# Chunk 0's reciprocal taken from VectorE in two halves, PSUM cleared by ScalarE, and a new order of all tasks, in a gated linear-attention and squared-ReLU kernel

## The chip, the cores and the metric

One core of a Trainium2 chip runs the whole program. The metric is the time of one execution in device microseconds; 338.8 us is the median of three runs before the change (338.04 to 339.99).

The engines are named as the profile names them: PE is TensorE (matmuls; PEld its weight loads), DVE VectorE, ACT ScalarE, POOL GpSimd, and SP the engine whose queue issues nearly all loads and stores.

## The reference

Two stages, for 4 batches of 768 tokens. First a gated linear attention with 8 heads of 48: a state per head decays by f and takes up k times v. Then a token mix, a squared-ReLU pair of products (384 to 1024 to 384), and a sigmoid gate.

```python
f = 1.0 / (1.0 + np.exp(-f_logit))
for t in range(S):
    state = f[:, :, t, :, None] * state + np.einsum('bhd,bhe->bhde', k[:, :, t], v[:, :, t])
    y[:, :, t] = np.einsum('bhd,bhde->bhe', q[:, :, t], state)
# x is y, heads side by side; x_prev is x one token earlier
xk = mu_k * x + (1.0 - mu_k) * x_prev
xr = mu_r * x + (1.0 - mu_r) * x_prev
k = np.maximum(xk @ w_k, 0.0)
out = 1.0 / (1.0 + np.exp(-(xr @ w_r))) * (k * k @ w_v)
```

## The kernel before

The attention is done in 24 chunks of 128 tokens (6 per batch). The rest is done in 8 units of 3 chunks (384 tokens).

For chunk i the tasks are, by the names that the order uses: `qk` and `v` load q, k and v; `b` is a scan over the tokens that gives the running product of the gates, in PSUM (tag pm), and `bl` keeps its last column. `ln` and `rb` (ScalarE, Ln and then Exp of its negative) give 1/b roughly, `n` and `iv` (VectorE) improve it by one Newton step, which leaves it with a negative sign. `q` multiplies q by b (VectorE), `k` multiplies k by minus 1/b in two operations of 256 columns (GpSimd or VectorE). `S` is the scores k times q (16 small matmuls into pss), `m` and `mg` copy and mask them, `TR` and `kt` transpose k and copy it to SBUF, `P` is k times v. `g`, `za`, `zb` and `T` carry the state from chunk to chunk: `g` is the gate of the whole last chunk, `za` the decayed state, `zb` and `T` add the two parts of P. `YA`, `YB` are the output's matmuls (into py) and `y` copies them, times -1, to x and stage; `w` is a small copy between YA and YB.

The work of unit u: `sp` spreads rows of two heads by DMA, `d`, `xm`, `xh`, `xl` mix the token with the one before and split it in two float32r parts; for unit 0, chunks 0 to 2, the mix is done on TensorE instead (`XM`, with the diagonal matrices dg and eg, which come from mu). `F` is a block of the first product (9 matmuls), `r`, `h`, `kk`, `l` square and split it, `R` and `lg` the gate's product, `sg` its sigmoid, `W` a block of the second product (12 matmuls, four blocks of the hidden width each), `o` the gated output, `out` its store. The weights come as 64-bit words and are made into float32r pairs on the chip, each piece in steps S, T, X, H, L (as `wkS0`), from the loads `wk0` to `wk7`, `wr0` to `wr3`, `wv0` to `wv5`.

At the end the kernel checks that nothing it has simplified matters: `c0` to `c14` load the weights' words again through two buffers, `cm` gathers them, `lo` reduces on VectorE, `lot` turns the result on TensorE (two transposes), `lom` makes a flag of it in four small VectorE operations, and `strong` reads the flag on every engine for a branch to a general version, not taken here.

What sets the order: a long string, ORDER, names all tasks in one sequence, with the engine after a slash where there is a choice. Each engine does its own tasks in this sequence. Buffers are given out in this sequence as well. `constants` and the clears ahead of it come first.

Of the kernel before, what the change touches and what calls it, by code (L numbers as in the profile page):

```python
# [51 lines left out]
f0.0 f0.1 sf0.0 b0 mu wv3 f0.2 sf0.1 sf0.2 f1 b1 sf1 ex wvS3/V wvT3 onemu wvX3 b2 bl0/V qk0 v0 qk1 bl2/A q0 bl1/V g2  # L52
dg/G b3 q1 ln0 rb0 ln1 bl3/V rb1 n0 iv0 wv2 qk2 n1 q2 iv1 k0/G k1/G wvS2/A qk3 q3 wvT2 wk0 ed2 v2 v1 wk4 S0 ln2 rb2
m0/A n2 wvX2 iv2 TR0 kt0/A wkS0/A S1 P0 zb0/A ln3 m1/A TR1 YA0 w0/A wkT0 wkX0 kt1/A rb3 T0 mg0/G g1 YB0 k2/G za1/G b4
n3 y0/A P1 S2 TR2 zb1 YA1 wk5 wk2 wk1 qk4 v3 ed0 ed1 wk6 wk3 iv3 T1 ln4 wkS5/A bl4/A m2/V wvH3/G mg1/G za2/G wkS2/A
kt2/A wkH0/A P2 rb4 w1/A wkS1/A wkT2 mg2/V wkT5 wkX2 q4 zb2 YB1 n4 T2 wkX5 wkT1 k3/G wkL0/G x00 wvH2/G g3 wkH5/G g4
# [119 lines left out]
class Rwkv:  # L176
# [10 lines left out]
    def b(self, *key):  # L187
        return self.tiles[key[0]][self.slot[key]]
# [12 lines left out]
    def add_attention(self, pl, i):  # L201
# [35 lines left out]
        def halves(t):  # L237
            return t[:, 1::2].rearrange("p a (h c) -> p a h c", h=2)
# [784 lines left out]
```

## Time and profile before

| | us |
|---|---|
| median of 3 runs | 338.8 |
| lowest, highest | 338.04, 339.99 |
| the profiled execution: own time | 339.45 |
| the profiled execution: span | 337.7 |
| TensorE busy | 309.6 (92%) |
| VectorE busy | 271.9 (81%) |
| ScalarE busy | 200.1 (59%) |
| GpSimd busy | 141.3 (42%) |

The profiled execution is one execution of the program. Its span is what the rows below show; 1.75 us of its own time lie around the span. The clock granted to TensorE was 0.998 of full speed over the span. An idle engine costs something only where another one, or the end, waits for it.

### The profile page before, as it was taken

The numbers are of one execution on the slowest core, as the hardware profiler recorded it, in microseconds if no ns is written. First come the engines' busy times: TensorE is split into PE (matmuls) and PEld (weight loads), VectorE is DVE, ScalarE is ACT, GpSimd is POOL, SyncE is SP. The second block draws the span as 40 slices with busy tenths as digits, with TensorE's granted clock in tenths as the row PEclk, the third lists the DMA queues.
The fourth block names the chain that finished last, engine by engine and source line by source line (L and its number), as shares of the span: only waits on it lengthen the run. The fifth ranks groups of instructions, "written<-read, shape, count | busy, mean of one in ns | idle before, by whom it ended". The sixth has DMA issues, their size and how long they took to land.

```text
span 337.7 us, 10736 instructions
## 1 busy us (share of the span) xinstructions
PE 309.6 (92%) x4458; PEld 296.5 (88%) x4458; DVE 271.9 (81%) x519; ACT 200.1 (59%) x427; POOL 141.3 (42%) x184
## 2 busy tenths in 40 slices
PE   0097989999999999999999999999999999999993
PEld 0076779999999998999999999999999999999893
DVE  8988889998799967599988958888889997663751
ACT  3786779776788246675975425656782532914150
POOL 2488878934426704231374424051434331113340
PEclk9999999999999999999999999999999999999999
DMA  7997949620025229300060607620065021326423
GB/s 246 384 264 237 318 127 411 214 107 2 1 90 170 92 53 365 120 1 2 14 203 22 209 2 215 199 82 0 2 211 156 4 64 48 112 68 213 136 99 105
DMA packets 20634, 45.32 MB, mean 134 GB/s; under 512 B 2848, under 2 KB 13024, under 8 KB 20576
## 3 DMA queue, kind: packets, MB, share of 16 engines
q1 hardware_dynamic: 20144, 43.96, 39.6%
q8 instruction: 37, 0.61, 0.8%
q10 hardware_dynamic: 432, 0.59, 0.5%
q14 instruction: 21, 0.17, 0.2%
HBM read 38.54 MB, written 4.72 MB: 128 GB/s over the span
## 4 chain that ended last, share of the span: by engine, by line
PE 82%; DMA 8%; DVE 3%; issue 3%; SPq 1%; POOL 1%; ACT 0%; DVEq 0%; POOLq 0%
PE pm L453 63%; PE py L334 8%; DMA qk<-in_qkt 4%; PE pss L302 4%; PE pm L287 3%; DMA words<-in_wk 3%; PE pm L583 2%; PE pss L321 2%; DMA out<-t 1%; DVE pm L525 1%; DVE t L545 1%; SPq L381 0%; POOL dg L761 0%; DVE dg L748 0%; DVE t L507 0%
## 5 line engine op out<-in xcount | busy, mean ns | idle before, releaser
L453 PE MATMUL pm<-xh,wk 128*128 128x384 f32 x384 | 104.8, 339 | 0.5 <-DVE t L629 0.5
L453 PE MATMUL pm<-wv,k2h 128*128 128x384 f32 x384 | 97.0, 333 | 0.4 <-DVE t L545 0.3
L453 PEld LDWEIGHTS pm<-xh,wk 128*128 128x128 f32 x384 | 69.3, 188 | 2.4 <-DVE t L629 0.8
L453 PEld LDWEIGHTS pm<-wv,k2h 128*128 128x128 f32 x384 | 68.3, 188 | 1.2 <-DVE t L545 0.6
L453 PE MATMUL pm<-wv,k2l 128*128 128x384 f32 x192 | 63.6, 331 | 0.0
L453 PE MATMUL pm<-xl,wk 128*128 128x384 f32 x192 | 63.6, 331 | 0.0
L635 POOL TENSOR_TENSOR k2l<-t,k2h 128x384 fp32r<-128x384 f32 x36 | 39.1, 1097 | 57.3 <-ACT k2h L627 44.7
L560 POOL TENSOR_TENSOR xl<-t,xh 128x384 fp32r<-128x384 f32 x25 | 26.4, 1064 | 59.8 <-ACT xh L553 42.6
L453 PE MATMUL pm<-wr,xh 128*128 128x384 f32 x144 | 36.5, 334 | 0.0
L453 PEld LDWEIGHTS pm<-xl,wk 128*128 128x128 f32 x192 | 36.1, 188 | 0.0
L453 PEld LDWEIGHTS pm<-wv,k2l 128*128 128x128 f32 x192 | 36.0, 188 | 0.0
L627 ACT ACTIVATE k2h<-t 128x384 fp32r<-128x384 f32 x64 | 32.5, 521 | 5.8 <-DVE t L623 5.6
L622 ACT ACTIVATE t<-pm 128x384 f32<-128x384 f32 x37 | 17.7, 489 | 30.6 <-PE pm L453 28.4
L302 PE MATMUL pss<-qk 64*64 64x64 f32 x768 | 17.2, 228 | 17.4 <-POOL qk L241 16.2
L302 PEld LDWEIGHTS pss<-qk 64*64 64x64 f32 x768 | 14.5, 141 | 18.4 <-POOL qk L241 16.2
L223 DVE TENSOR_TENSOR_SCAN pm<-f,low 128x512 f32<-128x512 f32 x24 | 30.2, 1262 | 0.2
L453 PEld LDWEIGHTS pm<-wr,xh 128*128 128x128 f32 x144 | 25.5, 188 | 0.2
L241 POOL TENSOR_TENSOR qk<-qk,rb 128x256 f32<-128x256 f32 x17 | 13.7, 806 | 27.2 <-DVE rb L246 27.1
L366 ACT ACTIVATE x<-py 64x128 f32<-64x128 f32 (+1 forms) x63 | 19.5, 309 | 9.1 <-PE py L334 8.1
L553 ACT CAST xh<-t 128x384 fp32r<-128x384 f32 x32 | 15.9, 511 | 14.9 <-DVE t L545 14.8
L545 DVE SCALAR_TENSOR_TENSOR t<-pm,mu_sb,x 128x384 f32<-128x384 f32 x42 | 24.2, 609 | 0.4
L453 PE MATMUL pm<-wr,xl 128*128 128x384 f32 x72 | 23.9, 332 | 0.0
(127 smaller groups left out, 597.9 us busy)
## 6 DMA issues: line engine op xcount, KB each, us to landing
qk<-in_qkt SPq DMA_DIRECT2D x24, 512.0 KB, 5.2
words<-in_wv SPq DMA_DIRECT2D x12, 512.0 KB, 5.0
f<-in_zt SPq DMA_DIRECT2D x7, 768.0 KB, 6.7
v<-in_vt SPq DMA_DIRECT2D x24, 192.0 KB, 3.8
out<-t SPq DMA_DIRECT2D x21, 192.0 KB, 4.1
words<-in_wk SPq DMA_DIRECT2D x6, 512.0 KB, 3.9
words_k2h<-in_wk SPq DMA_DIRECT2D x4, 384.0 KB, 6.4
words_k2l<-in_wk SPq DMA_DIRECT2D x4, 384.0 KB, 5.9
```

The lines of the kernel that those rows point to most:

```text
L223: pl.add(f"b{i}", ("V", lambda: nc.vector.tensor_tensor_scan(b().rearrange(FL), f().rearrange(FL), self.low.rearrange(FL), 1.0, op0=ALU.mu ...
L241: e.tensor_tensor(k()[:, ::2], k()[:, ::2], rb()[:, ::2], op=ALU.mult)
L302: nc.tensor.matmul(self.pss[HALF[h], r, 64 * j : 64 * j + 64], k()[HALF[r], j, HALF[h]], q()[HALF[r], j, HALF[h ^ j % 2]], start=True, sto ...
L334: first[c, h] = nc.tensor.matmul(to, lhs, rhs, start=(c, h) not in first, stop=stop, skip_group_check=True)
L366: e.activation(o, i_, AF.Copy, scale=-1.0)
L453: nc.tensor.matmul(lines(ps), lhs(a, j), lines(rhs(bb, j)), start=ends[0] and i == 0, stop=ends[1] and i == len(pr) - 1)
L545: pl.add(f"xm{u}.{p}{w}{j}", ("V", lambda xm=xm, w=w, j=j: nc.vector.scalar_tensor_tensor(xm(), pm("d", u, p, j), self.mu_sb[:, w, j : j + ...
L553: pl.add(f"xh{u}.{p}{w}{j}", ("A", lambda xm=xm, hi=hi: nc.scalar.copy(hi(), xm())), ("V", lambda xm=xm, hi=hi: nc.vector.tensor_copy(hi() ...
L560: e.tensor_tensor(lo(), xm(), hi().bitcast(F32), op=ALU.subtract)
L622: pl.add(f"r{name}", ("A", lambda: nc.scalar.activation(r(), ps(), AF.Relu)), ("V", lambda: nc.vector.tensor_scalar(r(), ps(), 0.0, None, ...
L627: pl.add(f"h{name}", ("A", lambda: nc.scalar.activation(hi(), r(), AF.Square)), after=[f"r{name}"], **(kw | {"uses": kw["uses"] + [("t", " ...
L635: e.tensor_tensor(lo(), kk(), hi().bitcast(F32), op=ALU.subtract)
```

## The change

For chunk 0 the running product b goes to SBUF (the tile lg, which is free at the start) instead of PSUM. Its reciprocal is taken by VectorE's own reciprocal, in two halves of two head pairs (`ra0`, `rb0`); `ln0`, the Exp, `n0` and `iv0` are gone. k's product follows in two halves on GpSimd (`ka0`, `k0`), of two operations with 128 columns each. Since this reciprocal has a positive sign, q of chunk 0 is negated first (`nq0`, ScalarE), and the gate of chunk 1 is negated (`g1`, now on VectorE). The scores of chunk 0 are two tasks (`Sa0`, `S0`) with two head pairs each. Two clears of PSUM that were memsets on VectorE are copies of zeros on ScalarE. ORDER is another string: 1407 words for 1406.

```diff
-        b = lambda: self.b("pm", ("b", i)).rearrange("p (a c) -> p a c", a=NP)
+        home = ("lg", "b0") if i == 0 else ("pm", ("b", i))
...
+            def turned(e):
+                e.scalar_tensor_tensor(g(), self.bl[:, 0], -1.0, f()[:, :, 0], op0=ALU.mult, op1=ALU.mult)
...
-        pl.add(f"S{i}", ("P", scores), after=I("q") + I("k") + I("m", i - 1))
+        if i == 0:
+            pl.add("Sa0", ("P", lambda: scores((0, 1))), after=["q0", "ka0"])
+            pl.add("S0", ("P", lambda: scores((2, 3))), after=["Sa0", "k0"])
+        else:
+            pl.add(f"S{i}", ("P", scores), after=I("q") + I("k") + I("m", i - 1))
...
+    def add_first(self, pl, q, k, b, rb, home):
+
+        nc = self.nc
+        pl.add("nq0", ("A", lambda: nc.scalar.activation(q(), q(), AF.Copy, scale=-1.0)), after=["qk0"])
+        pl.add("q0", ("G", lambda: nc.gpsimd.tensor_tensor(q(), q(), b(), op=ALU.mult)),
+               ("V", lambda: nc.vector.tensor_tensor(q(), q(), b(), op=ALU.mult)), after=["nq0"], uses=[home])
+        for n, js in (("ra0", slice(0, 2)), ("rb0", slice(2, 4))):
+            pl.add(n, ("V", lambda js=js: nc.vector.reciprocal(rb()[:, js].rearrange(FL), b()[:, js].rearrange(FL))),
+                   uses=[home] + ([("rb", 0)] if js.start else []), takes=[] if js.start else [("rb", 0)])
+
+        def k_rb(e, j):
+            e.tensor_tensor(k()[:, j], k()[:, j], rb()[:, j], op=ALU.mult)
+            t, r = (a[:, j + 1].rearrange("p (h c) -> p h c", h=2) for a in (k(), rb()))
+            e.tensor_tensor(t, t, r[:, ::-1], op=ALU.mult)
+
+        for n, j, ra in (("ka0", 0, "ra0"), ("k0", 2, "rb0")):
+            pl.add(n, ("G", lambda j=j: k_rb(nc.gpsimd, j)), ("V", lambda j=j: k_rb(nc.vector, j)),
+                   after=["qk0", ra] + (["ka0"] if j else []), uses=[("rb", 0)])
...
-    nc.vector.memset(k.py[:, :, :320], 0.0)
-    nc.vector.memset(k.pss[:, :, 256 : 256 + NP * D], 0.0)
+    zeros = k.eg.rearrange("p m j c -> p (m j c)")
+    for t, n in ((k.py[:, :, :320], 320), (k.pss[:, :, 256 : 256 + NP * D], NP * D)):
+        nc.scalar.copy(t, zeros[:, : 2 * n].rearrange("p (h c) -> p h c", h=2))
...
-f0.0 f0.1 sf0.0 b0 mu wv3 f0.2 sf0.1 sf0.2 f1 b1 sf1 ex wvS3/V wvT3 onemu wvX3 b2 bl0/V qk0 v0 qk1 bl2/A q0 bl1/V g2
+f0.0 sf0.0 f0.1 f0.2 sf0.1 f1 b0 qk0 b1 bl0/A sf0.2 sf1 nq0 ex ra0 b2 ka0/G rb0 k0/G TR0 bl1/A kt0/A ln1 rb1 q0/V v0 wv3 mu onemu qk1 b3 q1 n1 v1 qk2
```

Three places in the new order matter for what follows. In the rows below the first word is the line in each kernel, numbers behind names are buffers, and f, qk, words and pm stand for gates, q and k, weight words and PSUM.

VectorE near the start, before: from the scan of chunk 2 (L223) over q0 and q1 (L233) to the Newton steps n and iv of chunks 0 and 1 (L244, L246).

```order
L223 SCALAR_TENSOR_TENSOR pm_96<-f_61,low 128x512
L227 COPY bl<-pm_93 128x4
L233 TENSOR_TENSOR qk_64<-qk_64,pm_93 128x512
L227 COPY bl<-pm_94 128x4
L223 SCALAR_TENSOR_TENSOR pm_95<-f_62,low 128x512
L233 TENSOR_TENSOR qk_65<-qk_65,pm_94 128x512
L227 COPY bl<-pm_95 128x4
L244 TENSOR_TENSOR pm_93<-rb_97,pm_93 128x512
L246 SCALAR_TENSOR_TENSOR rb_97<-pm_93,rb_97 128x512
L244 TENSOR_TENSOR pm_94<-rb_98,pm_94 128x512
L233 TENSOR_TENSOR qk_66<-qk_66,pm_96 128x512
L246 SCALAR_TENSOR_TENSOR rb_98<-pm_94,rb_98 128x512
```

The same engine from its first scan in the changed kernel: scans (L228), the two reciprocals, q0 (L397), one minus mu (L794), q1, n1, T0 (L270) and iv1.

```order
L228 SCALAR_TENSOR_TENSOR lg_121<-f_61,low 128x512
L228 SCALAR_TENSOR_TENSOR pm_93<-f_61,low 128x512
L399 RECIPROCAL rb_97<-lg_121 128x256
L228 SCALAR_TENSOR_TENSOR pm_94<-f_61,low 128x512
L399 RECIPROCAL rb_97<-lg_121 128x256
L397 TENSOR_TENSOR qk_64<-qk_64,lg_121 128x512
L794 TENSOR_SCALAR one_mu<-mu_sb 128x6
L228 SCALAR_TENSOR_TENSOR pm_96<-f_62,low 128x512
L374 TENSOR_TENSOR qk_65<-qk_65,pm_93 128x512
L385 TENSOR_TENSOR pm_93<-rb_98,pm_93 128x512
L270 TENSOR_TENSOR sm<-pss,z_73 128x192
L387 SCALAR_TENSOR_TENSOR rb_98<-pm_93,rb_98 128x512
```

The Newton step of chunk 0 and three small copies have left this stretch; the reciprocals stand around the scan of chunk 2, one_mu stands between q0 and the scan of chunk 3, and T0 has come up ahead of iv1.

SP's queue of loads at the start, before:

```order
L381 DMA f_61<-in_zt 128x512 x2
L755 DMA mu_sb<-in_mu 128x6
L666 DMA words_122<-in_wv 128x1024
L381 DMA f_61<-in_zt 128x512
L381 DMA f_62<-in_zt 128x1536
L211 DMA qk_64<-in_qkt 128x1024
L213 DMA v_103<-in_vt 128x384
L211 DMA qk_65<-in_qkt 128x1024
```

And in the changed kernel:

```order
L419 DMA f_61<-in_zt 128x512 x3
L419 DMA f_62<-in_zt 128x1536
L211 DMA qk_64<-in_qkt 128x1024
L213 DMA v_103<-in_vt 128x384
L704 DMA words_122<-in_wv 128x1024
L793 DMA mu_sb<-in_mu 128x6
L211 DMA qk_65<-in_qkt 128x1024
L213 DMA v_104<-in_vt 128x384
```

The load of mu and the first piece of w_v have moved behind q, k and v of chunk 0.

TensorE near the program's end, before: the two transposes of the check (L789) and the read of the flag (L800), with the first and last rows of the one block of 12 matmuls between them, and the first of the block behind.

```order
L789 MATMUL pm_94<-ident,t_114 1x128 x2
L453 MATMUL pm_93<-wv_86,k2h_891 128x3x32x4
...
L453 MATMUL pm_93<-wv_86,k2l_978 128x3x32x4
L800 TENSOR_LOAD flag
L453 MATMUL pm_95<-wv_86,k2h_891 128x3x32x4
```

The same place in the changed kernel, with the last two matmuls of block W7.00 ahead:

```order
L491 MATMUL pm_96<-wv_87,k2h_846 128x3x32x4
L491 MATMUL pm_96<-wv_86,k2l_857 128x3x32x4
L827 MATMUL pm_95<-ident,t_114 1x128 x2
L838 TENSOR_LOAD flag
L491 MATMUL pm_94<-wv_86,k2h_846 128x3x32x4
L491 MATMUL pm_94<-wv_87,k2h_846 128x3x32x4
```

The read of the flag now follows the transposes directly, and four blocks (48 matmuls) stand behind it, where one stood before.

## Rows read from the trace of the kernel before

**Rows 1.** The page, part 1: busy us (share of span) x instructions.
```profile
PE 309.6 (92%) x4458; PEld 296.5 (88%) x4458; DVE 271.9 (81%) x519; ACT 200.1 (59%) x427; POOL 141.3 (42%) x184
```

**Rows 2.** Busy us by stretch: stretch, length, PE, PEld, DVE, ACT, POOL, clock, DMA, GB/s.
```profile
10.00:20.00 10.00, 3.58 (x84) 2.95 (x88) 9.21 (x17) 8.20 (x13) 6.66 (x9) 1.00 0.92 334
20.00:30.00 10.00, 7.16 (x251) 5.79 (x243) 8.43 (x18) 8.22 (x25) 8.37 (x13) 1.00 0.84 255
...
100.00:150.00 50.00, 50.00 (x788) 48.48 (x784) 39.51 (x75) 31.39 (x73) 18.23 (x24) 1.00 0.42 139
```

**Rows 3.** TensorE's waits, whole program: us, times, longest.
```profile
PE pss L302 <- POOL qk L241: 16.2, 1, 16.2
...
PE pss L321 <- issue: 1.7, 1, 1.7
```

**Rows 4.** The chain of waits, 3 to 47 us: start, length, what.
```profile
17.83 1.04 PE pm L287 x4
...
32.22 4.86 PE pm L583 x26
...
37.08 0.84 issue
...
43.59 1.65 issue
...
46.39 0.69 PE pm L453 x4
```

**Rows 5.** Timeline of VectorE, 0 to 32 us: start, length, operation, [idle before].
```profile
4.74 2.35 DVE L223 TENSOR_TENSOR_SCAN pm<-f,low 128x512 f32<-128x512 f32 x2
...
11.11 0.69 DVE L233 TENSOR_TENSOR qk<-qk,pm 128x512 f32<-128x512 f32 x1 [0.46 <-DMA qk<-in_qkt]
...
15.28 0.69 DVE L244 TENSOR_TENSOR pm<-rb,pm 128x512 f32<-128x512 f32 x1
...
15.88 0.68 DVE L233 TENSOR_TENSOR qk<-qk,pm 128x512 f32<-128x512 f32 x1
...
22.25 1.22 DVE L223 TENSOR_TENSOR_SCAN pm<-f,low 128x512 f32<-128x512 f32 x1
...
29.70 0.35 DVE L279 TENSOR_TENSOR sm<-pss,z 128x192 f32<-128x192 f32 x1
```

**Rows 6.** Timeline of ScalarE, same stretch.
```profile
3.52 1.28 ACT L387 ACTIVATE f<-f 128x512 f32<-128x512 f32 x2 [1.49 <-DMA f<-in_zt]
...
9.79 1.48 ACT L392 ACTIVATE f<-f 128x1536 f32<-128x1536 f32 x1 [1.24 <-DMA f<-in_zt]
...
12.65 0.60 ACT L229 ACTIVATE rb<-pm 128x512 f32<-128x512 f32 x1
...
13.28 0.63 ACT L231 ACTIVATE rb<-rb 128x512 f32<-128x512 f32 x1
```

**Rows 7.** Timeline of GpSimd, same stretch.
```profile
12.02 0.97 POOL L264 TENSOR_TENSOR g<-bl,f 128x4 f32<-128x4 f32 x1 [9.62 <-DVE bl L227]
...
15.45 0.73 POOL L241 TENSOR_TENSOR qk<-qk,rb 128x256 f32<-128x256 f32 x1 [0.89 <-DVE rb L246]
...
19.94 0.20 POOL L264 TENSOR_TENSOR g<-bl,f 128x4 f32<-128x4 f32 x1
```

**Rows 8.** Timeline of all engines around the flag, 326 to 333 us.
```profile
326.54 0.69 DVE L748 SCALAR_TENSOR_TENSOR dg<-words,dg 128x512 int32<-128x512 int32 x1 [2.28 <-DMA words<-in_wk]
...
327.80 0.52 PE L789 MATMUL pm<-ident,t 128*1 128x128 f32 x2
...
329.06 0.15 DVE L796 SCALAR_TENSOR_TENSOR flag<-t 1x1 int32<-1x1 f32 x1
...
329.79 1.60 ACTq L511 DMA_DIRECT2D out<-t  x2
...
332.51 0.56 DVE L507 TENSOR_TENSOR t<-pm,lg 128x384 f32<-128x384 f32 x1 [1.48 <-PE pm L453]
```

**Rows 9.** The chain of waits at the end: start, length, what.
```profile
328.32 4.10 PE pm L453 x24
```

More of the change, by code (lines that the diff above doesn't have):

```diff
@@ L51 @@
 ORDER = """
-f0.0 f0.1 sf0.0 b0 mu wv3 f0.2 sf0.1 sf0.2 f1 b1 sf1 ex wvS3/V wvT3 onemu wvX3 b2 bl0/V qk0 v0 qk1 bl2/A q0 bl1/V g2
[L53 to L56, printed above, removed]
@@ L126 @@
+c11 F7.07 r7.07/A kk7.07/A h7.01 cm1 l7.03/V h7.07 kk7.01/A kk7.05/A l7.01/G R7.2 F7.06 R7.1 r7.06/A kk7.06/A c7
+lg7.1/A cm7 cm11 lo l7.07/G W7.10 W7.00 out6.2 h7.06 lg7.2/A l7.05/G sg7 lot lom out3.0 out6.1 strong l7.06/G W7.20
+W7.11 o7.1 out7.1 W7.01 o7.0 W7.21 out7.0 o7.2 out6.0 out7.2
 """
@@ L293, in add_attention, with scores @@
                takes=[("ktk", i)], uses=[("pm", ("k", i))])
-        def scores():
-            for j in range(NP):
+        def scores(js=range(NP)):
+            for j in js:
                 for r in (0, 1):
@@ L371, in add_attention, with add_inverse, halves, k_rb @@
                after=I("YB"), **({"takes" if t0 == 0 else "uses": [("x", mu), ("stage", mu)]}))
+    def add_inverse(self, pl, i, I, q, k, b, rb):
+        nc = self.nc
+        pl.add(f"ln{i}", ("A", lambda: nc.scalar.activation(rb(), b(), AF.Ln)),
+               after=["ex"], takes=[("rb", i)], uses=[("pm", ("b", i))])
+        pl.add(f"rb{i}", ("A", lambda: nc.scalar.activation(rb(), rb(), AF.Exp, scale=-1.0)),
+               after=I("ln"), uses=[("rb", i)])
+        pl.add(f"q{i}", ("V", lambda: nc.vector.tensor_tensor(q(), q(), b(), op=ALU.mult)),
+               after=I("qk"), uses=[("pm", ("b", i))])
+        def halves(t):
+            return t[:, 1::2].rearrange("p a (h c) -> p a h c", h=2)
+        def k_rb(e):
+            e.tensor_tensor(k()[:, ::2], k()[:, ::2], rb()[:, ::2], op=ALU.mult)
+            e.tensor_tensor(halves(k()), halves(k()), halves(rb())[:, :, ::-1], op=ALU.mult)
+        pl.add(f"n{i}", ("V", lambda: nc.vector.tensor_tensor(b(), rb(), b(), op=ALU.mult)),
+               after=I("rb") + I("q") + I("bl"), uses=[("pm", ("b", i)), ("rb", i)])
+        pl.add(f"iv{i}", ("V", lambda: nc.vector.scalar_tensor_tensor(
+            rb(), b(), 2.0, rb(), op0=ALU.subtract, op1=ALU.mult)), after=I("n"), uses=[("pm", ("b", i)), ("rb", i)])
+        pl.add(f"k{i}", ("G", lambda: k_rb(nc.gpsimd)), ("V", lambda: k_rb(nc.vector)),
+               after=I("iv") + I("qk"), uses=[("rb", i)])
```

171 lines of the change are left out of this document (82 added, 89 removed).

## The prediction

> **What bounds the kernel now.** I read the page's busy times first, then the stretches, TensorE's waits, the chain of waits, and the timelines of the start and of the end. TensorE is busy 309.6 of 337.7 us [rows 1], and from 100 to 150 us it is never idle [rows 2]. Its waits say where the other 28 us are: 16.2 us ahead of its first score matmul, then 1.7 us in the middle of one group of matmuls where no engine was waited for [rows 3]. So matmuls are the bound, their number is the same in both kernels, and only the two ends of the program can give or take time. After the first weight product starts at 46.39 us [rows 4], TensorE hardly stops until its last product is read at 332.51 [rows 8].
>
> Up to 46.39 the chain [rows 4] shows slow groups (four transposes in 1.04 us), then the first token-mix matmuls (XM) at 32.22, and two gaps called "issue" (0.84 and 1.65 us) in which TensorE waited for nothing that the profile shows. Behind that start stands VectorE: its busy share is 9.21 and 8.43 us of 10 in the stretches from 10 to 30 us, against 3.58 and 7.16 for TensorE [rows 2]. VectorE's queue ends this phase with T2, the state sum of chunk 2, at 29.70 + 0.35 = 30.05 [rows 5]; XM follows 2.17 us later. I therefore count what the change does to VectorE's queue ahead of T2.
>
> **The change part by part, at the start.**
>
> *Clears.* The two PSUM clears leave VectorE, whose first scan began at 4.74 [rows 5]. The gate it needs was ready at about 4.16 (half of two sigmoids that start at 3.52 and take 1.28 [rows 6]), so only 0.5 us is gained: the scan starts at about 4.2. ScalarE waited 1.49 us for the gates' load just there [rows 6]; two copies of 640 and 384 columns, at the sigmoid's 0.64 us for 512, take 1.3 us. They fit and cost nothing; without that cover they would take back 0.5.
>
> *Loads.* mu and the first piece of w_v (515 KB together) move behind the first q/k load. Gates f1 were there at 9.79 [rows 6] and the 512 KB of q/k behind them at 11.11 [rows 5], 1.32 us for 512 KB, so q/k of chunk 0 should land at about 9.8.
>
> *Chunk 0.* GpSimd can start k as soon as q/k is there. Its first elementwise operation took 0.97 us on four columns, a later one of the same kind 0.20 [rows 7]: 0.77 us that now fall on the path. A k operation of 256 columns takes 0.73 [rows 7], so I estimate 0.37 for the new 128-column ones (not over 0.73). First half 9.8 + 0.77 + 0.74 = 11.3, second half 12.05, the last two transposes (half of 1.04 [rows 4]) 12.6, the copy to SBUF 13.1 (counted half a microsecond, under the Ln's 0.60), Ln and Exp of chunk 1 at 0.60 and 0.63 [rows 6] 14.35. TensorE's first work comes over 4 us earlier, but chunk 1 gains far less.
>
> *VectorE's queue.* A 512-column operation occupies it 0.60 us (starts at 15.28 and 15.88 [rows 5]). Out of the queue ahead of T2 go n0 and iv0 (no Newton step for chunk 0), one shift of w_v and one masking (both to ScalarE), and q4 and n4, now behind T2: six operations, 3.6 us. In come two half reciprocals and, net, one 384-column weight operation (at most 0.6). No row shows a reciprocal. The nearest rows are a 512-column product (0.60) and a 512-column scan (1.22 [rows 5]), so a half of 256 columns lies between 0.30 and 0.61; it reads one operand and carries no state, so I stay in the middle, 0.45. The queue shrinks by 3.6 - 0.6 - 0.9 = 2.1 us.
>
> *New waits on VectorE.* With scans at 1.17 (two in 2.35 [rows 5]) it is through both reciprocals at 4.2 + 3 x 1.17 + 0.9 = 8.6. q0 now waits for ScalarE's negation of q, which cannot end before 9.8 + 0.6 = 10.4: 1.8 us idle, with the scan of chunk 3 and q1 queued behind. one_mu then waits for mu, which sits behind v0 and the w_v piece (704 KB, 1.8 us at the rate above): 11.6, 0.6 us idle. Scan and q1 end at 13.4, and n1 waits for the Exp at 14.35: 0.95. That is 3.35 us of idling; before, VectorE was idle about 0.8 + 1.6 = 2.4 us from 10 to 30 [rows 2]. So 0.95 more.
>
> T2 then ends at 30.05 - 0.5 - 2.1 + 0.95 = 28.4, and XM, the same 2.17 us later, at 30.6: **1.65 us earlier**. Behind XM the same matmuls follow in another order (F0.01 ahead of P4), and I let both issue gaps recur. TensorE's first scores being in two tasks changes nothing by itself: the second half waits for nothing that the first doesn't, except k's second half, and the transposes ahead of it wait for that already.
>
> **The change at the end.** Whether the weights allow the fast path is computed on the chip: a reduction on VectorE, two transposes on TensorE, four small VectorE operations that write flag, and then every engine reads flag. Before, TensorE has twelve matmuls between its transposes and its read, and no gap is seen there. In the new order the read stands right behind the transposes, with 48 matmuls behind it (8.2 us, twice the 24 that close the chain [rows 9]). The transposes ended at 327.80 + 0.52 = 328.32, flag was written at 329.21, and ScalarE, which reads it too, went on at 329.79 [rows 8]. So TensorE must stand still for at least 0.6 us (0.89 less up to 0.3, since an output product no longer sits between the small operations) and at most 1.47 (with ScalarE's 0.58 for the read). I take **1.2 us**, nearer to the upper end because TensorE also has to read. Nothing covers it: TensorE is the bound there. On GpSimd the last residue operation is queued behind the read; it needs about 1.2 us while TensorE has a block of 2.05 us first, so it isn't late. On ScalarE only output loads to DRAM stand behind it, and on SP one output that was ready long before.
>
> **The sum.** 339.45 (the profiled execution's own time) - 1.65 + 1.2 = 339.0. That execution was 0.65 above the median of 338.8, so I expect a median of **338.3**, no change that can be told: a measurement of this kernel can tell about 0.5%, 1.7 us.
>
> [...]
>
> **Rivals.**
>
> [...]
>
> *The head gains more.* Both issue gaps come where TensorE works through many short instructions while the loads are heaviest, so other positions may avoid them. Without the 0.84 and the 1.65 the time is 338.3 - 2.5 = 335.8; with one of them left, 336.6 to 337.5. For it: the mix's tail is now followed by a wait for VectorE that can hide one. Against: the loads are as many.
>
> *No gain at the start.* If the loads and not VectorE set the pace up to 46 us, the head gains nothing and the end still costs 1.2: 340.0. For it: two issue gaps and a q/k load on the chain. Against: VectorE's share, and only 0.46 us of wait for q/k at 11.11 [rows 5].
>
> *Slower: the check comes too late.* Before, the last check word was worked on at 326.54, just as it landed [rows 8], 6 us ahead of TensorE's end, and 24 matmuls stood behind the transposes. Now 48 do, 4.1 us more. If the check words come as late as before, seen from the end, TensorE waits those 4.1 us as well: 342.4; with half of it, 340.4. It decides from the point at which the last word lands less than some 10 us ahead of the end. For it: the words have two buffers, so each load waits for the one two before it. Against: seven of the loads are left after the last but one unit's output products begin, not eight.
>
> **How the numbers follow.** Forecast 0.36 (338.3, by the bounds 336.9 to 339.3: head 1.2 to 2.0 with the reciprocal's ends and waits of half a microsecond either way, end 0.6 to 1.5; a seventh of it under 337.1), more gain 0.27, eight passes 0.13, no gain at the start 0.10, check too late 0.14. Faster by over 0.5% (under 337.1): 0.27 + 0.05 = 0.32. Slower by over 0.5% (over 340.5): 0.14 and a third of the no-gain case, 0.17. Within: 0.51. The range reaches to the case with nearly both gaps gone, 335.7, and to the light form of the late check, 340.7.
>
> **What would show it.** Right at the start: the first scan at 4.2, q0 at 10.4, T2 ending near 28.4, XM near 30.6. [...] Right at the end: a TensorE gap of about 1.2 us behind the two transposes, in front of the last four blocks. Wrong: XM's start unmoved, a new wait at a unit's first product, or no gap at the flag.

## The result: about 1% slower, and the profile after

| | before | after |
|---|---|---|
| median of 5 runs, us | 338.69 (336.89 to 339.99) | 342.53 (341.51 to 343.82) |
| profiled execution, us | 339.45 (span 337.7) | 342.69 (span 340.9) |
| end of the last matmul, on the span's clock | 332.40 | 334.96 |

The ratio is 1.0121, 95% interval 1.0077 to 1.0164. A second measurement of the same kernel beside later experiments (below, 13) gave 1.0086 (1.0050 to 1.0121). So the change costs some 3 to 4 us, where 338.3 (335.7 to 340.7) was predicted: wrong in sign and outside the range.

Page of after, part 1, the line that answers [rows 1]:

```profile
PE 313.6 (92%) x4458; PEld 298.7 (88%) x4458; DVE 269.6 (79%) x511; ACT 199.9 (59%) x427; POOL 155.2 (46%) x197
```

The stretches of [rows 2], and 30 to 40 us besides (stretch, length, PE, PEld, DVE, ACT, POOL, clock, DMA, GB/s):

```profile
10.00:20.00 10.00, 6.69 (x112) 4.70 (x112) 8.90 (x15) 8.28 (x18) 7.74 (x10) 1.00 0.98 359
20.00:30.00 10.00, 7.24 (x261) 6.06 (x262) 9.26 (x18) 8.22 (x22) 9.29 (x13) 0.97 0.67 215
30.00:40.00 10.00, 9.29 (x124) 8.10 (x117) 8.07 (x16) 6.96 (x19) 6.55 (x9) 0.86 0.99 354
100.00:150.00 50.00, 50.00 (x757) 48.38 (x757) 38.34 (x77) 27.80 (x65) 16.59 (x21) 1.00 0.38 127
```

TensorE's waits in after, beside [rows 3] (us, times, longest; L491 are the weight products):

```profile
PE pm L278 <- POOL qk L403: 11.5, 2, 11.1
PE pm L491 <- DVE t L667: 1.5, 1, 1.5
...
PE pm L491 <- DVE t L545: 1.4, 1, 1.4
...
PE pm L491 <- DVE flag L834: 1.4, 1, 1.4
```

Before, the waits ahead of weight products (there L453) were these:

```profile
PE pm L453 <- DVE t L629: 0.5, 1, 0.5
PE pm L453 <- DVE t L545: 0.3, 1, 0.3
```

TensorE begins at 11.07 us instead of 16.23, as the change means it to. But three waits of 1.4 to 1.5 us now stand ahead of weight products: two on VectorE's operations t in the middle of the program, and the flag. The timelines show their places. First, VectorE and TensorE between units 0 and 1:

```profile
77.21 2.04 DVE L228 TENSOR_TENSOR_SCAN pm<-f,low 128x512 f32<-128x512 f32 x1
79.28 0.69 DVE L374 TENSOR_TENSOR qk<-qk,pm 128x512 f32<-128x512 f32 x1
79.89 0.55 DVE L545 TENSOR_TENSOR t<-pm,lg 128x384 f32<-128x384 f32 x1
...
80.49 0.43 PE L491 MATMUL pm<-xh,wk 128*128 128x384 f32 x1 [1.41 <-DVE t L545]
```

The output product o0.2 (L545) reads the PSUM buffer of the last output matmuls, which end at 77.5; one weight product still runs, and the one behind it needs that buffer. In VectorE's queue a scan (b7) and q7 stand ahead of o0.2, and TensorE waits 1.41 us. Between units 4 and 5:

```profile
216.50 0.57 DVE L563 TENSOR_TENSOR pm<-x 128x384 f32<-128x384 f32 x1 [2.38 <-DMA x<-stage]
...
216.98 0.55 DVE L667 SCALAR_TENSOR_TENSOR t<-pm,t 128x384 f32<-128x384 f32 x1
...
217.58 0.62 PE L491 MATMUL pm<-wv,k2h 128*128 128x384 f32 x2 [1.46 <-DVE t L667]
```

Here kk4.05 (L667) is the last reader of a PSUM buffer that the first output matmul takes, and it is queued behind d5.01 (L563), which waited 2.38 us for a transfer. And the flag, beside [rows 8]:

```profile
324.81 0.38 PE L827 MATMUL pm<-ident,t 128*1 128x128 f32 x2
...
325.83 0.15 DVE L834 SCALAR_TENSOR_TENSOR flag<-t 1x1 int32<-1x1 f32 x1
326.56 0.59 PE L491 MATMUL pm<-wv,k2h 128*128 128x384 f32 x2 [1.37 <-DVE flag L834]
```

The account on the two spans starts at the first product with w_r (all of unit 0's products with w_k are done then), first before, then after:

```profile
62.04 0.52 PE L453 MATMUL pm<-wr,xh 128*128 128x384 f32 x2
```

```profile
60.45 0.61 PE L491 MATMUL pm<-wr,xh 128*128 128x384 f32 x2
```

It comes 1.59 us earlier, **-1.6**. TensorE's stalls behind that are 1.41 + 0.32 + 1.46 instead of 0.29 + 0.54 + 0.09, **+2.3**; the flag **+1.4**. That is +2.1, and the last matmul ends 2.56 later. The other 0.5 goes mostly with the restarts: matmuls overlap (one takes 0.33 us, the next starts 0.17 behind it), and the first ones behind a stall start later than usual, so this stall costs some 0.3 besides its length (30 matmuls around the one at 217.58 take 6.84 us; at 0.17 each and with the stall of 1.46 it would be 6.56). The remaining 0.7 of the span lies behind the last matmul: 5.94 us to the end instead of 5.26, with the last output's store landing 3.47 us after its issue instead of 2.45. In the profiles below this tail takes anything from 4.6 to 6.8 us, whatever the order, so I count it as scatter.

### The profile page after: what moved, and what is told of

Its sections match the earlier page's. It is cut to its first block, busy times and chain, and to the rows that moved or that the text cites. A ratio compares the mean times of both kernels' runs of the same rounds, so it can differ in the third digit from the quotient of the medians.

```text
span 340.9 us, 10748 instructions
## 1 busy us (share of the span) xinstructions
PE 313.6 (92%) x4458; PEld 298.7 (88%) x4458; DVE 269.6 (79%) x511; ACT 199.9 (59%) x427; POOL 155.2 (46%) x197
## 4 chain that ended last, share of the span: by engine, by line
PE 78%; DMA 7%; DVE 5%; ACT 4%; SPq 2%; issue 2%; POOL 0%; DVEq 0%
PE pm L491 61%; PE py L329 6%; PE pss L293 3%; PE pm L278 3%; DMA mu_sb<-in_mu 2%; DMA x<-stage 2%; PE pss L312 2%; DMA words_k2l<-in_wk 2%; PE pm L621 2%; DVE pm L228 1%; SPq L472 1%; DVE t L583 1%; ACT k2h L665 1%; SPq L419 0%; DVE qk L374 0%
## 5 line engine op out<-in xcount | busy, mean ns | idle before, releaser
L491 PE MATMUL pm<-xh,wk 128*128 128x384 f32 x384 | 104.1, 338 | 1.4 <-DVE t L545 1.4
L491 PE MATMUL pm<-wv,k2h 128*128 128x384 f32 x384 | 97.1, 333 | 2.8 <-DVE t L667 1.5
L491 PEld LDWEIGHTS pm<-xh,wk 128*128 128x128 f32 x384 | 69.2, 188 | 3.3 <-DVE t L545 1.7
L491 PEld LDWEIGHTS pm<-wv,k2h 128*128 128x128 f32 x384 | 68.2, 188 | 3.7 <-DVE t L667 1.8
L673 POOL TENSOR_TENSOR k2l<-t,k2h 128x384 fp32r<-128x384 f32 x41 | 44.9, 1108 | 45.0 <-DVE t L667 18.4
L491 PE MATMUL pm<-wv,k2l 128*128 128x384 f32 x192 | 63.6, 331 | 0.0
L491 PE MATMUL pm<-xl,wk 128*128 128x384 f32 x192 | 63.6, 331 | 0.0
L598 POOL TENSOR_TENSOR xl<-t,xh 128x384 fp32r<-128x384 f32 x30 | 32.6, 1097 | 55.8 <-DVE xh L592 28.6
L491 PE MATMUL pm<-wr,xh 128*128 128x384 f32 x144 | 36.6, 335 | 0.0
L491 PEld LDWEIGHTS pm<-xl,wk 128*128 128x128 f32 x192 | 36.1, 188 | 0.0
L491 PEld LDWEIGHTS pm<-wv,k2l 128*128 128x128 f32 x192 | 36.0, 188 | 0.0
L228 DVE TENSOR_TENSOR_SCAN pm<-f,low 128x512 f32<-128x512 f32 x23 | 32.5, 1416 | 0.1
L667 DVE SCALAR_TENSOR_TENSOR t<-pm,t 128x384 f32<-128x384 f32 x38 | 20.8, 551 | 7.6 <-ACT k2h L665 3.2
L278 PE MATMUL pm<-ident,qk 128*128 128x128 f32 x96 | 16.1, 291 | 11.6 <-POOL qk L403 11.5
L491 PEld LDWEIGHTS pm<-wr,xh 128*128 128x128 f32 x144 | 25.5, 188 | 0.3
L382 POOL TENSOR_TENSOR qk<-qk,rb 128x256 f32<-128x256 f32 x17 | 12.9, 759 | 27.8 <-DVE rb L387 17.1
L583 DVE SCALAR_TENSOR_TENSOR t<-pm,mu_sb,x 128x384 f32<-128x384 f32 x42 | 24.9, 610 | 0.6
L661 DVE TENSOR_SCALAR t<-pm 128x384 f32<-128x384 f32 x26 | 14.2, 553 | 13.2 <-PE pm L491 10.9
L329 PE MATMUL py<-qk,z 64*64 64x64 f32 x704 | 22.2, 231 | 2.1 <-DVE z L264 1.4
L491 PE MATMUL pm<-wr,xl 128*128 128x384 f32 x72 | 23.9, 332 | 0.0
```

What stands on the lines that cost most here:

```text
L228: pl.add(f"b{i}", ("V", lambda: nc.vector.tensor_tensor_scan(b().rearrange(FL), f().rearrange(FL), self.low.rearrange(FL), 1.0, op0=ALU.mu ...
L278: nc.tensor.transpose(pk()[:, j], k()[:, j], self.ident)
L329: first[c, h] = nc.tensor.matmul(to, lhs, rhs, start=(c, h) not in first, stop=stop, skip_group_check=True)
L382: e.tensor_tensor(k()[:, ::2], k()[:, ::2], rb()[:, ::2], op=ALU.mult)
L491: nc.tensor.matmul(lines(ps), lhs(a, j), lines(rhs(bb, j)), start=ends[0] and i == 0, stop=ends[1] and i == len(pr) - 1)
L583: pl.add(f"xm{u}.{p}{w}{j}", ("V", lambda xm=xm, w=w, j=j: nc.vector.scalar_tensor_tensor(xm(), pm("d", u, p, j), self.mu_sb[:, w, j : j + ...
```

## The experiments

All ratios are to the kernel before, measured in the same group, with 95% intervals; to set beside them, the changed kernel has 1.0121 and 1.0086.

| | kernel | ratio | interval |
|---|---|---|---|
| 1 | changed, flag read 24 matmuls later | 1.0027 | 0.9989 to 1.0064 |
| 2 | changed, o0.2 and kk4.05 earlier | 1.0020 | 0.9985 to 1.0055 |
| 3 | changed, y2 earlier | 1.0201 | 1.0145 to 1.0257 |
| 4 | before, flag read 12 matmuls earlier | 1.0077 | 1.0042 to 1.0112 |
| 5 | 1 and 2 together | 0.9955 | 0.9927 to 0.9982 |
| 6 | new start, old order from 63 us | 1.0190 | 1.0152 to 1.0228 |
| 7 | 3, with wkL5 on GpSimd | 1.0091 | 1.0060 to 1.0121 |
| 8 | new tasks in the old order | 1.0042 | 1.0007 to 1.0076 |
| 9 | new start, old order from 78 us | 0.9969 | 0.9941 to 0.9996 |
| 10 | old tasks in the new order | 1.0169 | 1.0112 to 1.0225 |
| 11 | 5, with iv18 earlier | 0.9951 | 0.9924 to 0.9978 |
| 12 | changed, copies for reciprocals | 1.0065 | 1.0033 to 1.0096 |
| 13 | changed, once more | 1.0086 | 1.0050 to 1.0121 |
| 14 | changed, clears on VectorE | 1.0062 | 1.0032 to 1.0092 |
| 15 | 1 once more | 1.0038 | 1.0005 to 1.0072 |
| 16 | 11, with the early read | 0.9999 | 0.9968 to 1.0029 |

My theory after the result was: three separate stalls that the new order made, each an operation queued behind something it needn't wait for. The rival: VectorE is late all through, so a stall that is taken away comes back further on.

### The flag's read (1, 4, 13, 15, 16)

```diff
 1, 15 (changed kernel):
-lom out3.0 out6.1 strong l7.06/G W7.20 W7.11 o7.1
+lom out3.0 out6.1 l7.06/G W7.20 W7.11 strong o7.1
 4 (kernel before):
-lot W7.11 o7.0 lom o7.1 strong out6.1
+lot lom strong W7.11 o7.0 o7.1 out6.1
```

> The changed kernel with one step moved: TensorE's read of the flag (and with it every engine's read) stands behind 24 of the 48 last matmuls instead of ahead of all 48; nothing else. Theory: in the changed kernel TensorE stood still for 1.37 us in front of the read (324.92 to 326.56 with the transposes' own share, 1.5 us); with 24 matmuls (4.1 us) between the transposes and the read, no gap is left there, so 342.5 - 1.5 = 341.0. Rival: the end is set by the last output's load to DRAM and by what the engines do after the read, so the gap is not worth its length and the time stays at 342.5.

> The kernel before with one part of the change alone: the flag's four small VectorE operations and the read stand right behind the two transposes, ahead of the last 24 matmuls; nothing else. Theory: TensorE stands still there for about 1.4 us as in the changed kernel (1.37 us), so 338.7 + 1.5 = 340.2. Rival: the read's wait is paid elsewhere in the order of the end (ScalarE's and SP's loads are issued earlier), and the time stays within half a microsecond of 338.7.

Experiment 1 measured 340.45 and experiment 4 341.93, the latter 2.6 above before. The read in 4 stands ahead of the last 24 matmuls instead of the last 12. TensorE's waits in 4 have the flag, those of 1 have no such line; in 4:

```profile
PE pm L453 <- DVE flag L796: 1.4, 1, 1.4
```

So the mechanism holds in both directions. The sizes were larger than the gap, with wide intervals, and the changed kernel rested on five runs; hence three more kernels in one group (16 is 11, below, with `strong` back in the place that the changed kernel gives it).

> The changed kernel itself, measured once more beside the others of this group, since its first five runs are the base of every difference so far. Theory (the traces' sum): against the kernel before it gains 2.1 us at the start and loses 1.6 + 1.6 in the middle, 1.5 at the flag and 0.7 behind the last matmul, less 1.4 of the waits of before that it doesn't have: ratio 1.006. Rival: the first five runs hold, ratio 1.012.

> The first experiment's kernel once more (the changed kernel with the flag's read behind 24 of the last 48 matmuls), beside the changed kernel in the same group. Theory: the difference is the gap that the trace shows, 1.5 us (ratio of the two 0.9955). Rival: it is 3 us as the first group's medians say (0.991), and something besides the gap goes with the read.

> The eleventh experiment with one step back: o0.2, kk4.05 and iv18 stay where they were moved to, but the flag's read stands ahead of all 48 last matmuls again, as in the changed kernel. Theory: 1.5 us above the eleventh experiment (ratio to before 0.9951), so 0.9995. Rival: 3 us above it, 1.004.

Within the group 13 measured 342.03 and 15 measured 340.45, 1.6 us apart; 16 lies 0.48% above 11, again 1.6 us. Each of these differences is known to some 1.5 us either way, but they agree with the trace: the price is its gap with the restart, about 1.5 us. The 3 us of the first medians were then scatter. 13 itself fell between theory and rival, and its interval reaches both.

### The two stalls in the middle (2, 5, 11)

```diff
-b7 q7 o0.2 ln7
+o0.2 b7 q7 ln7
-sp5.01 d5.01 kk4.05/V xm5.011
+sp5.01 kk4.05/V d5.01 xm5.011
 11 besides:
-n18 q19 iv18 n19
+n18 iv18 q19 n19
```

> The changed kernel with two steps moved on VectorE, nothing else: the output product o0.2 goes ahead of the scan b7 and of q7 (which stood in front of it), and kk4.05 goes ahead of d5.01 (which waits for a transfer between SBUF tiles). Theory: the two stalls of TensorE in the middle (1.41 us at 80.49 and 1.46 us at 217.58) are waits for a PSUM buffer that these two operations free, held up by what stands ahead of them in VectorE's queue; both go, and with them 1.56 + 1.62 = 3.2 us of TensorE's time: 339.3. Rival: VectorE is as late as before with other work, the stalls come back a few operations further on, and at most half is gained: 341 or more.

> The changed kernel with the moves of the first two experiments together (o0.2 ahead of the scan b7, kk4.05 ahead of d5.01, the flag's read behind 24 of the last 48 matmuls). Theory: the three stalls are separate costs, 1.5 + 1.6 + 1.6 us, and the new order of the start is worth some 2 us against the kernel before; so the sum is 342.5 - 4.7 + 0.7 (a stall that came back at 227 us) = 338.5, level with the kernel before or up to 1 us faster. Rival: the stalls share one cause (VectorE is late all through) and with two moved the rest grows: 340 or more.

> The fifth experiment (three moves) with one more: the Newton step iv18 goes ahead of q19 on VectorE. Theory: the stall of 0.33 to 0.53 us at 228 us is again a wait for a PSUM buffer, the one that iv18 reads last; 0.6 us earlier it is no wait: 338.1 - 0.5 = 337.6. Rival: the time stays at 338.1, since what TensorE gains there it loses at the next wait.

Two moved tasks gave 339.93 in experiment 2 (ratio 1.0020), against 342.5 and 342.0 for the changed kernel (1.0121 and 1.0086). In its waits t L545 and t L667 are gone, and one smaller wait has come in at 228 us:

```profile
PE pm L491 <- DVE flag L834: 1.4, 1, 1.4
...
PE pm L491 <- DVE rb L387: 0.5, 1, 0.5
```

With the read moved too, 5 measured 338.08, faster than the kernel before. 11 measured 337.79 and its wait at 228 us shrank to 0.14, but from 5 it can't be told. The rival falls for the most part: about a fifth of the gain came back. Both versions beat the kernel before, by 0.45 and 0.49%, and the changed kernel by more. The two swaps were not run apart; that each takes away its own stall is read from the trace of 2.

### Which part of the start gains (8, 9, 10, 6)

```diff
 8 (the changed code, order of before):
-b1 sf1 ... qk1 bl2/A q0 bl1/V g2 ... q1 ln0 rb0 ln1 ... rb1 n0 iv0 wv2 ... iv1 k0/G k1/G ... S0
+b1 ra0 rb0 sf1 ... qk1 bl2/A nq0 q0/V bl1/V ka0/G k0/G g2 ... q1 ln1 ... rb1 wv2 ... iv1 k1/G ... Sa0 S0
 10 (the code of before, new order):
-sf1 nq0 ex ra0 b2 ka0/G rb0 k0/G TR0 ... rb1 q0/V v0 ... dg/G Sa0 P0
+sf1 ex ln0 rb0 b2 q0 n0 iv0 k0/G TR0 ... rb1 v0 ... dg/G P0
 6: order of the changed kernel up to R0.2, the rest in the order of before
 9: order of experiment 5 up to rb7 (behind F1.02), the rest in the order of before
```

> The changed kernel's code in the order of the kernel before: ScalarE clears PSUM, chunk 0's reciprocal comes from VectorE in two halves (behind the second scan), its k from GpSimd as soon as q/k is there, the scores in two tasks; everything else in the old places. Theory: the start is gained by the new order, not by the new tasks: chunk 0 is ready earlier, but TensorE's next work waits for chunk 1's, so the time is 339 within a microsecond. Rival: what gains the start is that ScalarE's Ln and Exp and two VectorE operations of chunk 0 are gone; then most of the 2 us shows here too: 337.

> The kernel before's code in the new order: VectorE clears PSUM, chunk 0 has Ln, Exp, product and Newton step again (at the places of the two reciprocals), its scores are one task; everything else stands as in the changed kernel. Theory: the new order needs the reciprocal: the table of Ln and Exp is there only at 12.5 us, so chunk 0's k comes about 4 us later, chunk 1's Newton step 1.3 us, and the start loses 1.5 us against the changed kernel: ratio to before 1.016 to 1.018. Rival: VectorE and TensorE catch up before the mix, and the time is that of the changed kernel, ratio 1.012.

8 measured 341.20, by the ratio 0.4% above before; 10 measured 346.06, at the ratio expected, though its interval (1.0112 to 1.0225) holds the rival's 1.012 too. The traces say what each is worth at the start: the first product with w_r comes at 64.06 in both, against 62.04 and 60.75 in the two profiles of the old start (before, 4) and 60.45 in after. So at the start each half alone loses; only together do they gain. In 10 the loss against after is 3.6 us there, more than the 1.5 of the theory. In 8 both reciprocals, 3.34 us of VectorE, stand right behind the second scan, ahead of the rest of the start, and T2 ended at 32.70 instead of 30.05. So its theory was right that the tasks alone gain nothing, but not that they cost nothing.

> The changed kernel's code and its order up to the last product of unit 0 with w_r (about 63 us), and from there the order of the kernel before, the end with the flag included. Theory: the change's loss lies all in the new order behind 63 us, and its start is worth 1.6 to 2.5 us: 339.0 - 2.0 = 337.0. Rival: the start's gain is an effect of one profiled execution (the kernel before lost 0.84 and 1.65 us there in issue gaps that another profile of the same start did not show), so without the new order behind it the time is that of before, 339.

> The changed kernel's code and its order up to the first product of unit 1 (about 78 us; with o0.2 ahead of b7), and from there the order of the kernel before, the flag's end included. It repeats the sixth experiment (346.3) with the seam at a place where the two orders differ in one load and one check word only. Theory: the sixth lost 3.33 and 2.91 us at its seam (TensorE's waits at 73 and 77 us) and nothing else; here there is no such loss, and the start's 1.6 to 2.5 us remain to the end: 339.1 - 2.0 = 337.1. Rival: before's order needs its own start ahead of it, new stalls come at the seam or behind it, and the time is 339 or more.

6 measured 346.27, the clearest miss: its seam made a stall of the same kind as the others. VectorE and TensorE there:

```profile
71.78 0.57 DVE L563 TENSOR_TENSOR pm<-x 128x384 f32<-128x384 f32 x1 [6.01 <-DMA x<-stage]
...
72.91 0.55 DVE L673 TENSOR_TENSOR k2l<-t,k2h 128x384 fp32r<-128x384 f32 x1
...
73.52 0.44 PE L491 MATMUL pm<-wv,k2l 128*128 128x384 f32 x1 [3.33 <-DVE k2l L673]
```

A difference that waits 6.01 us for its transfer stands ahead of the residue that TensorE needs. A second stall, 2.91 us, ends at 77.73, and from 73.93 to 80.76 the granted clock was at its lower level (0.50 in after and 13; 0.986 over the span of 6). 9, with the seam at 78 us, measured 338.47, 0.3% under before: the sign of the theory, half its size (in its profile the first product with w_r came at 60.94, late for this start, and a wait of 0.67 stood at the seam).

### Parts of the start (3, 7, 12, 14)

```diff
 3:
-n4 wkS3/A wkH5/A wkS6/A wkT3 iv4 wkX3 y2/A wkH3/A XM0.00
+n4 y2/A wkS3/A wkH5/A wkS6/A wkT3 iv4 wkX3 wkH3/A XM0.00
 7: 3 and
-wkL5/V
+wkL5/G
 12:
-nc.vector.reciprocal(rb()[:, js]..., b()[:, js]...)
+nc.vector.tensor_copy(rb()[:, js]..., b()[:, js]...)
 14:
-nc.scalar.copy(t, zeros[:, : 2 * n]...)    # py and pss
+nc.vector.memset(k.py[:, :, :320], 0.0); nc.vector.memset(k.pss[:, :, 256 : 256 + NP * D], 0.0)
```

> The changed kernel with one step moved on ScalarE: y2 (the output of chunk 2 into the mix's input) goes ahead of the shift of two pieces of w_k, one of which waited 1.84 us for its load. Theory: the token mix's first group stops halfway, from 34.25 to 35.12, because y2 stands behind those shifts in ScalarE's queue; with y2 ahead the mix runs through and everything up to the first weight products comes 0.8 us earlier: 341.7. Rival: the first weight products wait for weights or for VectorE's part of the mix and not for the mix itself, so the start of the mix moves and the time doesn't: 342.5.

> The third experiment (y2 ahead of two weight shifts) with one more edit: the subtraction wkL5, which took 4.73 us on VectorE there and 0.83 in the changed kernel, goes to GpSimd at the same place. Theory: it took so long because VectorE's operation on three SBUF tiles got no turn while GpSimd ran one operation behind the other (its run ended at 50.83, the subtraction at 51.24); on GpSimd it takes about 1 us, the stall of 2.89 us at 53.01 goes, and the time falls by at least 3 us from 345.9, to 342 or less. Rival: the stall belongs to the order of the unit's first products, z is late for another reason, and the time stays within 1 us of 345.9.

3 measured 345.86, 3 to 4 us worse than the changed kernel instead of 0.8 better. The reason is in VectorE's and GpSimd's timelines:

```profile
45.86 1.29 POOL L304 TENSOR_TENSOR ss<-ss,mask 128x512 f32<-128x512 f32 x1
46.51 4.73 DVE L734 TENSOR_TENSOR wk<-words_k2h,wk 128x384 fp32r<-128x384 f32 x1
47.09 0.54 POOL L730 CAST wk<-words_k2l 128x384 fp32r<-128x384 f32 x1
47.58 0.68 POOL L730 CAST wv<-words 128x512 fp32r<-128x512 f32 x1
48.21 2.62 POOL L734 TENSOR_TENSOR wv<-words,wv 128x512 fp32r<-128x512 f32 x2
52.52 0.35 DVE L264 TENSOR_TENSOR z<-pss,z 128x192 f32<-128x192 f32 x1
53.01 0.46 PE L329 MATMUL py<-qk,z 64*64 64x64 f32 x16 [2.89 <-DVE z L264]
```

The subtraction wkL5 on VectorE, 0.83 us in the changed kernel, took 4.73: it began while GpSimd was in an operation and ended 0.41 us behind the last of an unbroken run on GpSimd (50.83). Behind the stall of 2.89 the granted clock was at its lower level as well, from 53.37 to 56.78 (0.995 over the span). With the subtraction on GpSimd (7) the time was 342.88, 3.0 lower; the second half of the theory ("342 or less") was missed by 0.9, and it stands where the changed kernel does. So y2's place gains nothing that these runs can tell, and the loss of experiment 3 goes with the subtraction's engine. That the cause is the two engines' contention is read from the two timelines; no run tests it apart from the move.

> The changed kernel with copies in place of the two half reciprocals (it leaves the reciprocal out, so chunk 0's k is wrong): each takes about 0.3 us and not 1.73. Theory: VectorE is through them 2.8 us earlier, but then waits for the negated q and for mu as before; only chunk 0's k would come earlier, and that waits for q/k, so nothing is gained behind the mix: within 0.5 us of the changed kernel, ratio 1.012. [...]

> The changed kernel with one part undone: the two PSUM clears are VectorE's again, ahead of its first scan. Theory: the first scan starts 0.5 to 0.7 us later (4.05 before), but VectorE then waits as long for the negated q at 11.2 us, so the time is that of the changed kernel. Rival: the second reciprocal ends later, chunk 0's second half with it, and the whole start moves by the same 0.6 us.

12 measured 341.80 (ratio 1.0065), 14 measured 340.99 (1.0062); the changed kernel's second ratio, 1.0086, lies in both intervals, its first in neither. 12's theory (ratio 1.012) missed, but the changed kernel itself was at 1.0086 when it was run again, so the ratios don't settle whether the reciprocals' length holds the start up. The trace leans that way: 12's first product with w_r came at 58.97, earlier than in any of ten profiles with the changed kernel's start (59.38 to 60.94). So the reciprocal's length may be worth about 1 us, and moving the clears gains nothing that can be told: in 14 the first scan starts at 4.73 instead of 4.05, but q0 starts at 11.35 instead of 11.22.

## Why the prediction was wrong, step by step

**The step that failed** is in its first part: "only the two ends of the program can give or take time". That was read from before, where TensorE hardly stops behind 46 us, and carried over to a kernel whose order was searched anew from end to end. I weighed the new order at the start and at the end alone. Two PSUM buffers in the middle are freed later in the new order. TensorE stalls 2.9 us for them, 2.3 more in the middle than before with the small stalls of either, which no rival had; experiment 2 moves the two operations and the stalls are gone. "Wrong: a new wait at a unit's first product" stood in the last part, as a sign, and neither the sum nor the range held it. "XM's start unmoved", another of the signs, came as well (below).

**The end: right.** 1.2 us (0.6 to 1.47) was predicted for TensorE's stand at the flag; the trace has 1.37, the two later pairs of runs 1.6 each, and experiment 4 2.6. The flag was written at 325.99 and TensorE went on at 326.56, 0.57 later, about what ScalarE's read was taken to be (0.58). "The check comes too late" did not happen: the last check word was done at 322.73, 2 us ahead of the transposes.

**The start: right in size by luck, wrong in its path.** 1.65 us was predicted; the traces give 1.6 at the first product with w_r. But profiles of one start differ: before had this product at 62.04, experiment 4, with the same order there, at 60.75; ten profiles with the changed kernel's start (after, 1, 2, 5, 6, 9, 11, 13, 15, 16) lie from 59.38 to 60.94, 60.1 in the mean. So the gain is about 1.3, or 0.6 to 1.9 by which profile of the old start is taken. The path was T2, then the mix (XM) 1.65 earlier. Of VectorE's head in after, beside [rows 5]:

```profile
4.05 1.22 DVE L228 TENSOR_TENSOR_SCAN lg<-f,low 128x512 f32<-128x512 f32 x1 [0.41 <-ACT f L425]
...
6.31 1.73 DVE L399 RECIPROCAL rb<-lg 128x256 f32<-128x256 f32 x1
...
11.22 0.76 DVE L397 TENSOR_TENSOR qk<-qk,lg 128x512 f32<-128x512 f32 x1 [0.47 <-ACT qk L395]
12.61 0.17 DVE L794 TENSOR_SCALAR one_mu<-mu_sb 128x6 f32<-128x6 f32 x1 [0.63 <-DMA mu_sb<-in_mu]
12.69 1.88 DVE L228 TENSOR_TENSOR_SCAN pm<-f,low 128x512 f32<-128x512 f32 x1
...
15.08 0.68 DVE L385 TENSOR_TENSOR pm<-rb,pm 128x512 f32<-128x512 f32 x1
...
28.77 0.36 DVE L270 TENSOR_TENSOR sm<-pss,z 128x192 f32<-128x192 f32 x1
```

- Clears: the scan at 4.05 (predicted 4.2), hidden on ScalarE as said, but by 14 the 0.5 us was worth nothing that can be told: the wait for the negated q takes it back.
- q/k of chunk 0 came at about 10.5, not 9.8; q0 at 11.2 (10.4), one_mu at 12.6 (11.6), n1 at 15.1 (14.35). q0 follows from the load, 0.7 late. n1 did not wait for the Exp, as the prediction had it (that ended at 14.91): one_mu came 1.0 late with its own load, and the scan behind it took 1.88 us instead of 1.17, beside GpSimd's products for dg (13.45 to 15.19).
- The reciprocal took 1.73 us a half, where 0.30 to 0.61 was the bound, and VectorE spent on it the time in which it was to wait for q and mu (it was idle for 1.84 us from 10 to 30, where 3.35 was forecast). So the queue ahead of T2 did not shrink by 2.1: the two reciprocals take back more than that. Each is 5.8 times the 0.30 that half of a 512-column product takes. How many passes a reciprocal makes, to which the forecast gave a chance of 0.13 ("eight passes"), no run shows; the runs showed 1.73 us a half, here and in 14, and 3.34 for the two in 8.
- T2 ended at 29.13, 0.9 earlier and not 1.65; XM began at 32.08, **unmoved** (before: 32.15). Between T2 and XM lay 2.95 us, not 2.17, with the granted clock at 0.50 from 29.4 to 32.8, behind a wait of 1.45 us: the 32 products ahead of XM took 1.01 us instead of 0.56. In the other profiles of this start the delay goes with the clock: where it fell there (1, 5, 9, 11, 15; 0.984 to 0.992 over the span) XM came 2.79 to 3.13 us behind T2, where it stayed at full speed (2, 6, 13, 16; 0.999 and 0.998 over the span of 2 and 16) 2.15 or 2.16, as predicted. T2 itself lay from 28.94 to 30.11 in them.
- Then the gain came on the other side of XM. I let both issue gaps (0.84 and 1.65) recur; in after neither is there. That is the condition of the rival "the head gains more". But in experiment 4, with the old start, neither is there either: it has an issue gap of 0.25 and a wait of 0.56 for ScalarE. So not the new order alone takes them away. The chain beside [rows 4]:

```profile
27.56 6.67 DMA words_k2l<-in_wk
...
34.77 0.31 ACT x L361
...
35.12 6.39 PE pm L621 x40
...
42.96 1.68 PE pm L491 x9
...
46.43 0.69 PE pm L491 x4
```

The first block of weight products (42.96, x9) is done before [rows 4] has the first one begin (46.39). XM stopped halfway for y2, which stood on ScalarE behind a load of w_k (0.71 us); by experiments 3 and 7 this stop costs nothing that the runs can tell.

**The sum:** 339.45 - 1.65 + 1.2 came out right in both terms (-1.6 and +1.4 measured), the first by luck, and lacked the middle, +2.3, some 0.5 of restarts, and the scatter of the tail, +0.7.

## What to carry to other kernels

Where an order is searched anew, the ends are not all: compare at every unit's boundary which operation frees the PSUM buffer that TensorE's next product takes, and what stands ahead of that operation in its engine's queue. An operation that waits for a transfer, or a long scan, in front of a buffer's last reader can stall TensorE (1.46 and 1.41 us in after); here one moved task each took it away. And before a gain at the start is booked, look at a second profile of the same start: the two issue gaps of 0.84 and 1.65 us that looked like its fixed costs were not there in experiment 4, and its first product with w_r came 1.3 us earlier.

## What the runs showed of the hardware

**A stall can cost more than its length.** In the second profile of the changed kernel (13) the stall at unit 5 was 2.05 us instead of 1.46, and the granted clock, 1.00 in the first profile, fell behind it to 0.50 for 3.4 us (217.5 to 220.9). The stretches of 13, and of after below:

```profile
215.00:220.00 5.00, 2.95 (x11) 2.65 (x10) 3.62 (x7) 4.61 (x5) 1.02 (x1) 0.75 0.66 216
220.00:225.00 5.00, 5.00 (x28) 5.00 (x27) 3.92 (x8) 1.49 (x2) 2.02 (x2) 0.91 0.67 258
```

```profile
215.00:220.00 5.00, 3.54 (x21) 3.23 (x20) 3.40 (x7) 4.46 (x6) 1.01 (x1) 1.00 0.68 227
220.00:225.00 5.00, 5.00 (x31) 5.00 (x30) 4.97 (x9) 2.38 (x4) 2.04 (x2) 1.00 0.75 277
```

From 215 to 225 us TensorE issued 39 matmuls in 13 and 52 in after; at 0.17 us a matmul that is 2.2 us, for a stall that is 0.6 longer. In experiment 14 a stall of 1.89 at the same place did not pull the clock down (0.998 over its span, 0.994 over that of 13). From the 20th matmul ahead of this stall to the 100th behind it 14 took 22.3 us and 13 took 24.1, with a stall 0.16 longer, so the fall itself cost 1.6 us. The length of a stall alone does not decide: the wait of 1.45 us near 29 us was followed by a clock of 0.50 in after, and not in 2, 6 and 13, where it was as long.

**VectorE operations took longer beside GpSimd's.** The 4.73 us of experiment 3, for 0.83 in after, are one case. In after, the scan b7 (77.21) took 2.04 us with GpSimd's residues beside it until 78.15, part of the stall at 80.49; in experiment 2, where it starts as GpSimd's residues end, it took 1.22. In both cases VectorE's operation ended only behind GpSimd's: the subtraction at 51.24 behind 50.83, the scan at 79.25 behind 78.15. In experiment 3 this went on over five of GpSimd's instructions in a row (45.86 to 50.83), though VectorE's operation began during the first, at 46.51.
